# One activation table named for a softmax and the inverse root behind it, and seven steps of the weight differences one slot apart in place of two

## The chip, the cores and the metric

The kernel runs on one core of a Trainium2 chip. The metric is the device time of one execution in microseconds, from the first to the last instruction and what the launch adds around them; times given for a kernel are the median of several runs. In the profile the engines are called PE (TensorE, matmul), PEld (its weight loads), DVE (VectorE), ACT (ScalarE), POOL (GpSimd) and SP (SyncE, which issues the DMAs here).

## The reference

A transformer block with parallel branches: the input, plus sliding-window attention of its layer norm, plus a dense layer with Mish, also of the layer norm.

```python
x = A_x                                   # 1 x 2048 x 576
xn = _layernorm(x, axis=-1)
# attention: 32 heads of 18, window of 8 keys, 2 positions apart
qkv = xn @ wqkv
logits = einsum(q, k at pos - 2*w) * scale ; masked where pos - 2*w < 0
attn = _softmax(logits, axis=-1)
a = (attn @ v) @ wo
# dense -> Mish -> dense, 4608 wide
h = xn @ w1 + b1
act = h * tanh(softplus(h))
b = act @ w2
return x + a + b
```

All of it is in float32.

## The kernel before, in words

**Two halves of tokens.** The 2048 tokens are worked in two halves (`hf` 0 and 1) of 1024, each in two blocks of 512. Every float32 operand of a matmul is split into a high part, cast by ScalarE (`copy` to float32r), and a low part, the difference that VectorE or GpSimd subtracts; a product is then three matmuls. To save matmuls the first dense layer, the output projection and a part of the q/k/v projection are computed in a Strassen-like way, from sums and differences of blocks of the weights and of the tokens.

**The plan.** Everything is put into a list of slots, `plan`. A slot holds TensorE's work of one step: `q` and `z` (q/k/v projection), `m` (first dense layer, `m1_part`: 512-wide products into `h` banks), `p` (second dense layer, `m2_pair`: two `po` tiles of 24 matmuls together, each then added to the accumulator `acc` by VectorE in `add_out`, L663). There are two `po` buffers, so the third of a row of `po` tiles waits until VectorE has read the first. One index `q` of the dense layers takes ten slots, six `m` and four `p` in turn; `spot(hf, q, i)` is the i-th of them. Other work is hung on slots with `before(slot, function)`. When the plan is written out, a slot first runs what is in `soon` (left there by the slot ahead), then what was hung on it, then its own work with what was held back (`pend`, the Mish activations of the products). Each engine runs its instructions in exactly the order in which they are written out.

**Attention** runs beside the dense layers, in steps that are spread evenly over the slots (`attention`, a generator). For a pair of heads GpSimd multiplies q with the keys (`pr`, L474), VectorE reduces to logits `L` (L479), adds a mask, subtracts the maximum, ScalarE takes the exponential (L497, through `soon`), VectorE normalises (L501 to L503), GpSimd multiplies with the values (`pv`, L510) and VectorE reduces that to `og` (L516). Behind the exponential of pair 4 of the first half, `root1` (L126) takes the inverse roots of the second half's variances: a logarithm (L127) and an exponential (L128) of eight values for each partition.

**Activation tables.** ScalarE holds one set of activation functions at a time. The program that builds the kernel puts an ACT_TABLE_LOAD ahead of an activation whose function is not in the set that was loaded last. A set can also be named and loaded explicitly (`preload_act_table_set`, used at L46). Mish (L618) is in another set than the exponential, so there is a load ahead of the softmax's exponential and one ahead of the next Mish.

**The weight differences.** In the second half, groups 2 and 3 of the q/k/v projection use differences of blocks of `wqkv` (`z_part`): with row halves 1 and 2 and column groups 2 and 3 as B11 to B22, T3 = B22 - B12, T1 = B12 - B11, T2 = B22 - T1 and T4 = B21 - T2 (`ZT`, L313). They are made during the first half, for two sets of rows (k = 0, 1). A difference has these steps: `z_load` (a DMA), `z_sum` (GpSimd, L335), `z_high` (ScalarE's cast, L339), `z_low` (VectorE, L343, in place), `z_keep` (two DMAs to DRAM, L347 and L348). T1, T2 and T4 are written over B12, B22 and B21, so the rows call them `zB`; the high parts are `zhT`. All these tiles come from a pool of five, `xn`. A table (L1109 to L1113) says which steps go where: entry n stands on slot `spot(0, 9, 4) + 30 * k + 2 * n` (L1116). Entries 10 to 16 are, in order: write T1; sum T4 and high T2; low T2; high T4; low T4; write T2; write T4.

Of the kernel before, what the change touches and what calls it, by code (L numbers as in the profile page):

```python
# [36 lines left out]
def block_kernel(ctx: ExitStack, tc: tile.TileContext, x, wq, wo, w1, b1, w2, mask, out):  # L37
    nc = tc.nc
# [91 lines left out]
    def newton1():  # L130
        newton(rs1, ve1, y1, nc.gpsimd)
        nc.gpsimd.tensor_mul(nm1, mv1[:, :, 0:1], rs1)
        nc.gpsimd.tensor_scalar(nm1, nm1, -1.0, None, op0=ALU.mult)
# [294 lines left out]
    def load_kv(hf, i, part):  # L428
        g, u = divmod(i, UQ)
        t = sb.tile([P, TJ + HALO, CU], F32, tag="kv", bufs=4, name=f"kv{part}_{hf}_{i}")  # L430
        src = kv_d[g][part * UQ + u, hf * SH, 0:1]
        nc.sync.dma_start(
            t.rearrange("p t c -> p (t c)"),
            bass.AP(tensor=src.tensor, offset=src.offset, ap=[[TJ * CU, P], [1, (TJ + HALO) * CU]]))
        return t

    def load_kq(hf, i):
        g, u = divmod(i, UQ)
        k = load_kv(hf, i, 0)
        q = sb.tile([P, TJ, CU], F32, tag="q", bufs=2, name=f"q_{hf}_{i}")  # L440
        nc.sync.dma_start(q, q_d[g][u, hf * SH:(hf + 1) * SH, :]
                          .rearrange("(p j) c -> p j c", j=TJ))
        return k, q

    def win(kv, c0, cn, j0, jn):
        base = kv[:, j0, c0:c0 + 1]
        return bass.AP(tensor=base.tensor, offset=base.offset,
                       ap=[list(base.ap[0]), [CU, jn], [DIL * CU, W], [1, cn]])

    pend, soon = [], []  # L450

    def attention(hf):
        kqs = [load_kq(hf, k) for k in range(PU)]
        yield
        behind = [None]

        def flush():
            if behind[0] is not None:
                behind[0]()
                behind[0] = None  # L460

        for pair in range(NQ * UQ // PU):
            n = f"{hf}_{pair}"
            vs, nxt = [], []
            L = sb.tile([P, PU, TJ, W, 2], F32, tag="L", bufs=2, name=f"L_{n}")
            hj = TJ // 2
            for k, (kt, q) in enumerate(kqs):
                for c in range(2):
                    flush()
                    pr = sb.tile([P, hj, W, CU], F32, tag="pr", bufs=2, name=f"pr_{n}_{k}_{c}")  # L470
                    j0 = c * hj
                    hh = hj // 2
                    for x in range(0, hj, hh):
                        nc.gpsimd.tensor_tensor(  # L474
                            out=pr[:, x:x + hh], in0=q[:, j0 + x:j0 + x + hh, None, :].to_broadcast([P, hh, W, CU]),
                            in1=win(kt, 0, CU, j0 + x, hh), op=ALU.mult)

                    def red(pr=pr, k=k, j0=j0, L=L):
                        nc.vector.tensor_reduce(  # L479
                            L[:, k, j0:j0 + hj].rearrange("p j w h -> p (j w h)"),  # L480
                            pr.rearrange("p j w (h d) -> p (j w h) d", h=2), axis=AX, op=ALU.add)
                    behind[0] = red
                    if k == 0:
                        vs.append(load_kv(hf, pair * PU + c, 1))
                    yield
            flush()
            if hf == 0:
                lm = L[0:2].rearrange("p k j w h -> p k (j w h)")
                nc.vector.tensor_add(lm, lm, mk[:, None, :].to_broadcast([2, PU, TJ * W * 2]))
            m = sb.tile([P, PU * TJ, 2], F32, tag="m", bufs=2, name=f"m_{n}")  # L490
            Lf = L.rearrange("p k j w h -> p (k j) w h")
            Lt = Lf.rearrange("p j w h -> p j h w")
            nc.vector.tensor_reduce(m, Lt, axis=AX, op=ALU.max)
            mb = m[:, :, None, :].to_broadcast([P, PU * TJ, W, 2])
            nc.vector.tensor_sub(Lf, Lf, mb)
            Ls = L.rearrange("p k j w h -> p (k j w h)")
            soon.append(lambda Ls=Ls: nc.scalar.activation(Ls, Ls, AF.Exp, scale=SCALE))  # L497
            if (hf, pair) == (0, 4):
                soon.append(root1)
            yield  # L500
            nc.vector.tensor_reduce(m, Lt, axis=AX, op=ALU.add)  # L501
            nc.vector.reciprocal(m, m)
            nc.vector.tensor_mul(Lf, Lf, mb)  # L503
            og = sb.tile([P, TJ, PU * CU], F32, tag="og", bufs=1, name=f"og_{n}")
            for k, vt in enumerate(vs):
                for h in range(2):
                    flush()
                    pr = sb.tile([P, TJ, DH, W], F32, tag="pr", bufs=2, name=f"pv_{n}_{k}_{h}")
                    for x in range(0, TJ, hj):
                        nc.gpsimd.tensor_tensor(  # L510
                            out=pr[:, x:x + hj].rearrange("p j d w -> p j w d"),
                            in0=L[:, k, x:x + hj, :, h:h + 1].to_broadcast([P, hj, W, DH]),
                            in1=win(vt, h * DH, DH, x, hj), op=ALU.mult)

                    def red(pr=pr, og=og, c0=k * CU + h * DH, last=(k, h) == (PU - 1, 1), pair=pair):
                        nc.vector.tensor_reduce(og[:, :, c0:c0 + DH], pr, axis=AX, op=ALU.add)  # L516
                        if last:
                            nc.sync.dma_start(
                                o_d[hf][:, pair * PU * CU:(pair + 1) * PU * CU]
                                .rearrange("(p j) c -> p j c", j=TJ), og)  # L520
                    behind[0] = red
                    if (hf, pair, k, h) == (0, 4, 0, 1):
                        newton1()
                    if k == 0 and (pair + 1) * PU + h < NQ * UQ:
                        nxt.append(load_kq(hf, (pair + 1) * PU + h))
                    yield
            kqs = nxt
        flush()
        yield
# [386 lines left out]
    def before(i, fn):  # L916
        plan[max(i, 0)][1].append(fn)
# [154 lines left out]
    def spot(hf, q, i):  # L1072
        return at["s", hf, q, i]

    for q in range(NP):
        if q == 0:
            i = at["q", 0, 3, 1, 0]
            ps_ = dict(raw=i - 3, sums=i - 1, wa=i, wc=i + 1, t0=i + 2, t1=i + 4)
        elif q == 1:
            i = at["q", 0, 3, 0, 0]  # L1080
# [15 lines left out]
    i = spot(0, NP - 1, 0)  # L1096
# [5 lines left out]
    i = at["q", 1, 0, 1, 1]  # L1102
# [4 lines left out]
    i = spot(0, 9, 4)  # L1107
    for k in range(2):
        for n, steps in enumerate((  # L1109
# [4 lines left out]
            for kind, name in steps:  # L1114
                f = dict(l=z_load, s=z_sum, h=z_high, o=z_low, k=z_keep)[kind]
                before(i + 30 * k + 2 * n, lambda f=f, name=name, k=k: f(name, k))  # L1116
    for q in range(NP):
        if q == 0:
            i = at["z", JB - 1, 0]
            ps_ = dict(wa=i - 7, t0=i - 6, t1=i - 5, wc=i - 4)  # L1120
        elif q == 1:
            i = spot(1, 0, 0)
# [9 lines left out]
    i = at["q", 0, 1, 1, 0]  # L1132
# [3 lines left out]
    i = at["q", 0, 3, 1, 0]  # L1136
# [5 lines left out]
    i = at["q", 1, 0, 1, 1]  # L1142
    for n in range(8):
        c, k = divmod(n, 4)
# [7 lines left out]
    for n in range(0, JB, 2):  # L1152
        i = at["q", 0, 1, 0, n]
# [4 lines left out]
    for n in range(TJ):  # L1158
        i = spot(0, 2 + n, 2)
# [3 lines left out]
    i = spot(0, NP - 2, 0)  # L1163
# [26 lines left out]
    def spread(hf, a, b):  # L1190
        before(a - 4, lambda: (att.__setitem__(hf, attention(hf)), next(att[hf])))
        k = a - 1
        for n in range(ASTEPS + 1):
            t = T[a] + n * (T[b] - T[a]) / (ASTEPS + 1)
            k = next(k for k in range(k + 1, len(plan)) if T[k + 1] > t and ok[k])
            before(k, lambda: next(att[hf], None))
# [5 lines left out]
    i = spot(1, NP - 1, 0)  # L1202
# [77 lines left out]
```

## Time and profile before

| what | value |
|---|---|
| median of 3 runs | 1140.36 us (1140.2 to 1140.48) |
| the profiled execution | 1140.93 us |
| its span, first to last instruction | 1138.8 us |
| mean granted TensorE clock | 0.997 |
| ACT_TABLE_LOADs, mean | 1283 ns |

Of these loads 16 stand ahead of a Mish (L618), 15 ahead of a softmax's exponential (L497), and one each at L46, L127 and L128. A row of a timeline has the start in us from the start of the span, the duration, the engine and line, what it writes and reads, shapes and a count of merged instructions; in brackets stands how long the engine was idle ahead of it and what ended that. Buffer numbers are left out in rows of the trace.

### The profile page before, as it was taken

The numbers are of one execution on the slowest core, as the hardware profiler recorded it, in microseconds if no ns is written. First come the engines' busy times: TensorE is split into PE (matmuls) and PEld (weight loads), VectorE is DVE, ScalarE is ACT, GpSimd is POOL, SyncE is SP. The second block draws the span as 40 slices with busy tenths as digits, with TensorE's granted clock in tenths as the row PEclk, the third lists the DMA queues.
The fourth block names the chain that finished last, engine by engine and source line by source line (L and its number), as shares of the span: only waits on it lengthen the run. The fifth ranks groups of instructions, "written<-read, shape, count | busy, mean of one in ns | idle before, by whom it ended". The sixth has DMA issues, their size and how long they took to land.

```text
span 1138.8 us, 17953 instructions
## 1 busy us (share of the span) xinstructions
PE 1125.9 (99%) x6726; PEld 1038.2 (91%) x6726; DVE 738.4 (65%) x1017; ACT 474.1 (42%) x845; POOL 725.9 (64%) x593
## 2 busy tenths in 40 slices
PE   8999999999999899999999999999999999999998
PEld 7998999989999799999999899999999999999998
DVE  6366777788887778877534265554555555556876
ACT  5544544354544535455232432324233342324332
POOL 2487877676689586885683475565664657577432
PEclk9999999999999999999999999999999999999999
DMA  6898767665668576666685984455535454653263
GB/s 203 279 316 306 245 242 262 240 233 211 216 223 303 192 279 228 235 253 211 204 302 179 295 325 167 161 184 210 187 136 191 148 210 144 236 197 105 88 215 110
DMA packets 126923, 246.87 MB, mean 217 GB/s; under 512 B 28754, under 2 KB 66932, under 8 KB 126836
## 3 DMA queue, kind: packets, MB, share of 16 engines
q1 hardware_dynamic: 126836, 245.72, 61.8%
q8 instruction: 53, 0.87, 0.3%
q14 instruction: 34, 0.28, 0.1%
HBM read 148.29 MB, written 97.39 MB: 216 GB/s over the span
## 4 chain that ended last, share of the span: by engine, by line
PE 94%; DVE 3%; ACT 1%; DMA 1%; issue 1%; SPq 0%; DVEq 0%; ACTq 0%
PE po L674 39%; PE h L595 29%; PE pq L289 11%; PE h L601 5%; PE o L828 4%; PE z L387 3%; DVE acc L663 0%; DMA acc<-in_x 0%; PE ta L73 0%; DVE L L479 0%; PE ot L709 0%; PE ot L725 0%; DVE st L110 0%; DVE t L253 0%; DMA kept_w<-w 0%
## 5 line engine op out<-in xcount | busy, mean ns | idle before, releaser
L674 PEld LDWEIGHTS po<-w,act 128*128 128x128 f32 x3456 | 476.2, 189 | 17.2 <-DVE acc L663 6.1
L674 PE MATMUL po<-w,act 128*128 128x288 f32 x3456 | 485.0, 296 | 4.5 <-DVE acc L663 4.4
L663 DVE TENSOR_TENSOR acc<-po,acc 128x576 f32<-128x576 f32 x288 | 215.8, 755 | 178.9 <-PE po L674 176.6
L621 POOL TENSOR_TENSOR act<-c,act 128x512 fp32r<-128x512 f32 x108 | 140.5, 1301 | 224.7 <-ACT act L620 202.1
L474 POOL TENSOR_TENSOR pr<-q,kv 128x576 f32<-128x576 f32 x128 | 191.6, 1520 | 33.0 <-DMA q<-q_d 27.4
L510 POOL TENSOR_TENSOR pv<-L,kv 128x576 f32<-128x576 f32 x128 | 175.7, 1466 | 30.9 <-DVE L L503 20.1
L606 ACT COPY c<-h 128x512 f32<-128x512 f32 x108 | 63.4, 587 | 223.5 <-PE h L601 137.9
L618 ACT ACTIVATE c<-c,b1c 128x512 f32<-128x512 f32 x108 | 78.3, 725 | 178.3 <-DVE c L617 177.8
L289 PE MATMUL pq<-wq,xt 128*128 128x432 f32 x672 | 136.4, 361 | 1.9 <-ACT xt L79 1.8
L289 PEld LDWEIGHTS pq<-wq,xt 128*128 128x128 f32 x672 | 125.0, 188 | 8.8 <-ACT xt L79 2.8
L617 DVE TENSOR_TENSOR c<-h,c 128x512 f32<-128x512 f32 x108 | 74.0, 687 | 72.3 <-PE h L601 36.6
L595 PE MATMUL h<-S,t 128*128 128x512 f32 x432 | 111.3, 393 | 0.0
L595 PE MATMUL h<-xt,t 128*128 128x512 f32 x432 | 110.7, 391 | 0.2 <-DVE c L617 0.2
L595 PE MATMUL h<-xt,wa 128*128 128x512 f32 x432 | 104.2, 390 | 0.0
L595 PEld LDWEIGHTS h<-xt,wa 128*128 128x128 f32 x432 | 81.0, 188 | 17.1
L479 DVE TENSOR_REDUCE L<-pr 128x64 f32<-128x1152 f32 x64 | 85.8, 1341 | 15.9 <-POOL pr L474 15.7
L595 PEld LDWEIGHTS h<-xt,t 128*128 128x128 f32 x432 | 79.2, 188 | 15.5 <-DVE c L617 0.7
L516 DVE TENSOR_REDUCE og<-pv 128x144 f32<-128x1152 f32 x64 | 85.8, 1340 | 8.0 <-POOL pv L510 7.9
L595 PEld LDWEIGHTS h<-S,t 128*128 128x128 f32 x432 | 77.3, 188 | 13.3
L620 ACT CAST act<-c 128x512 fp32r<-128x512 f32 x108 | 67.1, 621 | 4.7 <-PE po L674 0.3
L595 PE MATMUL h<-S,wc 128*128 128x512 f32 x216 | 55.9, 394 | 0.0
L621 POOL TENSOR_TENSOR act<-mn,act 128x512 fp32r<-128x512 f32 x36 | 48.1, 1335 | 6.1 <-ACT act L620 4.7
(179 smaller groups left out, 1235.3 us busy)
## 6 DMA issues: line engine op xcount, KB each, us to landing
kv<-kv_d SPq DMA_DIRECT2D x64, 396.0 KB, 5.7
kept_w<-w SPq DMA_DIRECT2D x36, 576.0 KB, 5.8
w<-kept_w SPq DMA_DIRECT2D x36, 576.0 KB, 5.9
kept_t<-t SPq DMA_DIRECT2D x36, 512.0 KB, 4.8
t<-kept_t SPq DMA_DIRECT2D x36, 512.0 KB, 6.2
rw<-in_w SPq DMA_DIRECT2D x36, 320.0 KB, 4.3
kept_wa<-wa SPq DMA_DIRECT2D x18, 640.0 KB, 6.5
wa<-kept_wa SPq DMA_DIRECT2D x18, 640.0 KB, 5.1
```

The lines of the kernel that those rows point to most:

```text
L289: nc.tensor.matmul(pq[:, 0:432], XT[:, xi, tok], wt[wi][:, hl, 0:432], start=i == 0, stop=i == len(seq) - 1)
L474: nc.gpsimd.tensor_tensor(out=pr[:, x:x + hh], in0=q[:, j0 + x:j0 + x + hh, None, :].to_broadcast([P, hh, W, CU]), in1=win(kt, 0, CU, j0 + ...
L479: nc.vector.tensor_reduce(L[:, k, j0:j0 + hj].rearrange("p j w h -> p (j w h)"), pr.rearrange("p j w (h d) -> p (j w h) d", h=2), axis=AX, ...
L510: nc.gpsimd.tensor_tensor(out=pr[:, x:x + hj].rearrange("p j d w -> p j w d"), in0=L[:, k, x:x + hj, :, h:h + 1].to_broadcast([P, hj, W, DH]),
L516: nc.vector.tensor_reduce(og[:, :, c0:c0 + DH], pr, axis=AX, op=ALU.add)
L595: nc.tensor.matmul(ph, wt[:, wl, wk * P:(wk + 1) * P], X[:, xs, :], start=first and i == 0, stop=last and i == len(seq) - 1, skip_group_ch ...
L617: nc.vector.tensor_tensor(out=t, in0=ph, in1=t, op=ALU.add)
L618: nc.scalar.activation(t, ph if fresh else t, AF.Mish, bias=b1c[:, f:f + 1])
L620: nc.scalar.copy(a[:, 0, :], t)
L621: nc.gpsimd.tensor_tensor(out=a[:, 1, :], in0=t, in1=a[:, 0, :].bitcast(F32), op=ALU.subtract)
L663: nc.vector.tensor_add(t.rearrange("p (c d) -> p c d", c=2), po[:, :, 0:HC], t.rearrange("p (c d) -> p c d", c=2))
L674: nc.tensor.matmul(po[:, c, 0:HC], acts[hf, q, b, j][:, al, tok], done["w2", hf, 2 * q + j][:, wl, c * HC:(c + 1) * HC], start=i == 0, sto ...
```

## The change

Two edits. For pair 4 of the first half, the table set that holds both the logarithm and the exponential is loaded by name ahead of the softmax's exponential. And for k = 0, entries 10 to 16 of the table stand on the slots `i` + 19, 20, 22, 23, 25, 26 and 27 in place of 20, 22, 24, 26, 28, 30 and 32. For k = 1 nothing moves.

```diff
             Ls = L.rearrange("p k j w h -> p (k j w h)")
+            if (hf, pair) == (0, 4):
+                soon.append(lambda: nc.scalar.preload_act_table_set("natural_log_exp_and_others"))
             soon.append(lambda Ls=Ls: nc.scalar.activation(Ls, Ls, AF.Exp, scale=SCALE))
             if (hf, pair) == (0, 4):
                 soon.append(root1)
...
                 f = dict(l=z_load, s=z_sum, h=z_high, o=z_low, k=z_keep)[kind]
-                before(i + 30 * k + 2 * n, lambda f=f, name=name, k=k: f(name, k))
+                before(i + (30 + 2 * n if k else 2 * n if n < 10 else (19, 20, 22, 23, 25, 26, 27)[n - 10]), lambda f=f, name=name, k=k: f(name, k))
```

The two added lines move the numbers of all later lines by 2 in rows of the changed kernel.

In ScalarE's rows around pair 4's softmax (L_0_4 are its logits, rs1 and ve1 belong to the inverse root, c21 and c22 are products that wait for Mish, zhT2 and zhT4 the high parts of T2 and T4) there stood before:

```order
L252 CAST wc_0_12_4058<-rw1_25_3889 128x384
L606 COPY c22_0_11_4105<-h1_0_11_3978 128x512
L339 CAST zhT2_0_4108<-zB22_0_3537 128x432
...
L252 CAST t1_0_12_4145<-tt1_12_3962 128x512
L497 ACT_TABLE_LOAD
L497 ACTIVATE L_0_4_3780<-L_0_4_3780 128x256
L127 ACT_TABLE_LOAD
L127 ACTIVATE rs1_104<-ve1_105 128x8
L128 ACT_TABLE_LOAD
L128 ACTIVATE rs1_104<-rs1_104 128x8
L618 ACT_TABLE_LOAD
L618 ACTIVATE c21_0_11_4052<-c21_0_11_4052,b1c_122 128x512
```

and now:

```order
L252 CAST wc_0_12_4061<-rw1_25_3889 128x384
L339 CAST zhT2_0_4065<-zB22_0_3537 128x432
L608 COPY c22_0_11_4108<-h1_0_11_3978 128x512
...
L252 CAST t1_0_12_4146<-tt1_12_3962 128x512
L339 CAST zhT4_0_4152<-zB21_0_3968 128x432
L498 ACT_TABLE_LOAD
L499 ACTIVATE L_0_4_3780<-L_0_4_3780 128x256
L127 ACTIVATE rs1_104<-ve1_105 128x8
L128 ACTIVATE rs1_104<-rs1_104 128x8
L620 ACT_TABLE_LOAD
L620 ACTIVATE c21_0_11_4055<-c21_0_11_4055,b1c_122 128x512
```

The two loads ahead of L127 and L128 are gone. T2's cast has moved ahead of one COPY, and T4's, which stood behind the next Mish and two casts of w2, has moved ahead of the softmax's table load.

In VectorE's rows from that softmax to the acc addition of the pair `po_0_11_1` (w2, wa and t1 are low parts of weights, og the reduction of pv) there stood before:

```order
L253 TENSOR_TENSOR t1_0_12_4145<-tt1_12_3962,t1_0_12_4145 128x512
L343 TENSOR_TENSOR zB22_0_3537<-zB22_0_3537,zhT2_0_4108 128x432
L617 TENSOR_TENSOR c21_0_11_4052<-h3_0_11_4006,c21_0_11_4052 128x512
...
L663 TENSOR_TENSOR acc_0_0_3_173<-po_0_10_0_3_4190,acc_0_0_3_173 128x576
L501 TENSOR_REDUCE m_0_4_4153<-L_0_4_3780 128x32
...
L516 TENSOR_REDUCE og_0_4_4209<-pv_0_4_0_0_4210 128x8x18
L253 TENSOR_TENSOR w2_0_24_4227<-rw2_24_4095,w2_0_24_4227 128x576
L617 TENSOR_TENSOR c11_0_12_4262<-h2_0_12_4264,c11_0_12_4262 128x512
L253 TENSOR_TENSOR wa_0_13_4276<-rw1_26_4147,wa_0_13_4276 128x640
L343 TENSOR_TENSOR zB21_0_3968<-zB21_0_3968,zhT4_0_4235 128x432
L663 TENSOR_TENSOR acc_0_1_0_183<-po_0_11_1_0_4292,acc_0_1_0_183 128x576
```

and now:

```order
L253 TENSOR_TENSOR t1_0_12_4146<-tt1_12_3962,t1_0_12_4146 128x512
L619 TENSOR_TENSOR c21_0_11_4055<-h3_0_11_4006,c21_0_11_4055 128x512
...
L665 TENSOR_TENSOR acc_0_0_3_173<-po_0_10_0_3_4193,acc_0_0_3_173 128x576
L343 TENSOR_TENSOR zB21_0_3968<-zB21_0_3968,zhT4_0_4152 128x432
L503 TENSOR_REDUCE m_0_4_4156<-L_0_4_3780 128x32
...
L518 TENSOR_REDUCE og_0_4_4213<-pv_0_4_0_0_4214 128x8x18
L253 TENSOR_TENSOR w2_0_24_4231<-rw2_24_4098,w2_0_24_4231 128x576
L619 TENSOR_TENSOR c11_0_12_4267<-h2_0_12_4269,c11_0_12_4267 128x512
L253 TENSOR_TENSOR wa_0_13_4281<-rw1_26_4148,wa_0_13_4281 128x640
L665 TENSOR_TENSOR acc_0_1_0_183<-po_0_11_1_0_4299,acc_0_1_0_183 128x576
```

T4's low part (zB21) no longer stands between og and the acc addition but ahead of the softmax's sum. T2's low part (zB22) has left this stretch; it stands some rows earlier, ahead of the addition to c22.

In SyncE's queue, from the write of w2_23, there stood before:

```order
L260 DMA kept_w2_23_4320<-w2_0_23_4204 128x1152
L260 DMA kept_w2_24_4336<-w2_0_24_4227 128x1152
L197 DMA rw2_25_4338<-in_w2 128x576
L347 DMA kept_T2_0_4343<-zhT2_0_4108 128x432
L348 DMA kept_T2_0_4343<-zB22_0_3537 128x432
...
L260 DMA kept_wa_13_4380<-wa_0_13_4276 128x1280
L197 DMA rw2_26_4383<-in_w2 128x576
L347 DMA kept_T4_0_4395<-zhT4_0_4235 128x432
L348 DMA kept_T4_0_4395<-zB21_0_3968 128x432
```

and now:

```order
L347 DMA kept_T2_0_4239<-zhT2_0_4065 128x432
L348 DMA kept_T2_0_4239<-zB22_0_3537 128x432
L432 DMA kv0_0_11_4252<-kv_d2_128 128x792
L441 DMA q_0_11_4254<-q_d2_132 128x288
L260 DMA kept_t1_12_4278<-t1_0_12_4146 128x1024
L347 DMA kept_T4_0_4283<-zhT4_0_4152 128x432
L348 DMA kept_T4_0_4283<-zB21_0_3968 128x432
L260 DMA kept_w2_23_4327<-w2_0_23_4207 128x1152
```

The writes of T2 and T4 have moved ahead of the write of w2_23. T1's pair of writes has moved likewise, ahead of the write of w2_22 and one load (rw2_23). On GpSimd and TensorE the order of instructions is the same as before.

## The prediction

> **What bounds the kernel.** I read the page's busy times first, then TensorE's waits, then the timeline around the longest of them.
>
> ```profile
> span 1138.8 us, 17953 instructions
> ...
> PE 1125.9 (99%) x6726; PEld 1038.2 (91%) x6726; DVE 738.4 (65%) x1017; ACT 474.1 (42%) x845; POOL 725.9 (64%) x593
> ```
>
> TensorE is busy for all but 12.9 us of the span. No other engine reaches two thirds. An edit that adds or removes no matmul can therefore gain only where TensorE waits or runs slowly.
>
> ```profile
> PE po L674 <- DVE acc L663: 4.4, 2, 4.2
> PE pq L289 <- ACT xt L79: 1.8, 2, 1.2
> ```
>
> (Who waited for whom: us in total, times, longest.) One wait of 4.2 us is by far the longest. Here it is in TensorE's timeline (start, duration, engine and line; in brackets the idle time ahead and what ended it):
>
> ```profile
> 371.82 3.35 PE L674 MATMUL po<-w,act 128*128 128x288 f32 x24
> 375.01 1.55 PE L595 MATMUL h<-xt,t 128*128 128x512 f32 x6
> ...
> 386.44 3.35 PE L674 MATMUL po<-w,act 128*128 128x288 f32 x24
> 389.62 1.54 PE L595 MATMUL h<-S,t 128*128 128x512 f32 x6
> 395.37 5.66 PE L674 MATMUL po<-w,act 128*128 128x288 f32 x24 [4.20 <-DVE acc L663]
> 400.87 1.55 PE L595 MATMUL h<-S,t 128*128 128x512 f32 x6
> ...
> 402.73 3.35 PE L674 MATMUL po<-w,act 128*128 128x288 f32 x24
> ```
>
> TensorE stops at 395.37 - 4.20 = 391.17: the pair at 386.44 filled both po buffers, and the next pair needs the first of them read by VectorE's acc addition. The reader should also see a second cost: the 24 matmuls behind the gap take 400.87 - 395.37 = 5.50 us, the same 24 at 371.82 take 375.01 - 371.82 = 3.19. That is 2.31 us more. The windows say why (span of the window, its length, busy time of each engine with instruction counts, granted TensorE clock, DMA share, GB/s):
>
> ```profile
> 5.00:10.00 5.00, 2.77 (x21) 2.16 (x19) 3.13 (x13) 4.28 (x12) 3.73 (x6) 1.00 1.02 359
> 391.00:392.00 1.00, 0.17 (x1) 0.00 (x0) 1.00 (x2) 0.00 (x0) 0.92 (x2) 1.00 0.00 0
> 393.00:394.00 1.00, 0.00 (x0) 0.00 (x0) 1.00 (x2) 0.97 (x3) 1.00 (x1) 0.74 1.10 378
> 399.00:400.00 1.00, 1.00 (x6) 1.00 (x5) 0.41 (x1) 0.00 (x0) 1.00 (x1) 0.50 0.94 364
> 400.00:401.00 1.00, 1.00 (x8) 1.00 (x7) 0.00 (x0) 0.00 (x0) 1.00 (x2) 0.84 1.09 271
> ```
>
> The clock halves inside 393 to 394 (0.74 there, so at about 393.5, 2.3 us into the gap) and returns at about 400.3. **The gap thus costs 4.20 + 2.31 = 6.51 us**, and that is the most that this change can give.
>
> **What makes the gap.** VectorE first, since its acc addition ends the wait:
>
> ```profile
> 372.64 0.69 DVE L617 TENSOR_TENSOR c<-h,c 128x512 f32<-128x512 f32 x1 [0.54 <-ACT c L606]
> ...
> 379.11 0.60 DVE L343 TENSOR_TENSOR zB<-zB,zhT 128x432 fp32r<-128x432 f32 x1
> ...
> 380.23 1.41 DVE L663 TENSOR_TENSOR acc<-po,acc 128x576 f32<-128x576 f32 x2
> 381.56 0.41 DVE L501 TENSOR_REDUCE m<-L 128x32 f32<-128x256 f32 x1
> ...
> 382.38 0.43 DVE L503 TENSOR_TENSOR L<-L,m 128x256 f32<-128x256 f32 x1
> ...
> 389.24 1.35 DVE L516 TENSOR_REDUCE og<-pv 128x144 f32<-128x1152 f32 x1 [2.48 <-POOL pv L510]
> 390.51 1.29 DVE L253 TENSOR_TENSOR w<-rw,w 128x576 fp32r<-128x576 f32 x1
> ...
> 393.06 1.58 DVE L343 TENSOR_TENSOR zB<-zB,zhT 128x432 fp32r<-128x432 f32 x1
> 394.57 1.41 DVE L663 TENSOR_TENSOR acc<-po,acc 128x576 f32<-128x576 f32 x2
> ...
> 397.16 0.67 DVE L253 TENSOR_TENSOR t<-tt,t 128x512 fp32r<-128x512 f32 x1
> ```
>
> From 389.24 on VectorE works without a pause up to the acc addition at 394.57, and one step of that run is T4's low part (the zB row at 393.06). The run starts late because the og reduction at 389.24 waits for GpSimd's pv product. GpSimd and ScalarE:
>
> ```profile
> 384.85 1.30 POOL L621 TENSOR_TENSOR act<-c,act 128x512 fp32r<-128x512 f32 x1 [8.73 <-ACT act L620]
> 386.10 3.10 POOL L510 TENSOR_TENSOR pv<-L,kv 128x576 f32<-128x576 f32 x2
> ...
> 392.36 3.40 POOL L510 TENSOR_TENSOR pv<-L,kv 128x576 f32<-128x576 f32 x2
> ```
>
> ```profile
> 372.02 0.59 ACT L606 COPY c<-h 128x512 f32<-128x512 f32 x1 [4.05 <-PE h L601]
> 372.50 0.56 ACT L339 CAST zhT<-zB 128x432 fp32r<-128x432 f32 x1
> ...
> 375.28 1.28 ACT L497 ACT_TABLE_LOAD   x1
> 378.62 0.42 ACT L497 ACTIVATE L<-L 128x256 f32<-128x256 f32 x1 [2.06 <-DVE L L495]
> 379.06 1.28 ACT L127 ACT_TABLE_LOAD   x1
> ...
> 380.58 1.28 ACT L128 ACT_TABLE_LOAD   x1
> ...
> 382.10 1.28 ACT L618 ACT_TABLE_LOAD   x1
> ...
> 384.15 0.62 ACT L620 CAST act<-c 128x512 fp32r<-128x512 f32 x1
> ```
>
> GpSimd's pv stands behind an act product that waits 8.73 us for ScalarE's cast at 384.15, and that cast stands behind four table loads, three of them back to back from 379.06.
>
> **The change, part by part.**
>
> *Table loads.* The order rows show the loads ahead of L127 and L128 gone, the first one still ahead of the exponential. The loads leave 2 x 1.28 = 2.56 us. Cast, act product, pv and og reduction start 2.56 earlier: og at 389.24 - 2.56 = 386.68. Late next is VectorE's L at 382.38, which pv also needs: it has 386.10 - 2.56 - (382.38 + 0.43) = 0.73 us to spare.
>
> [...]
>
> *T4's low part* (moved from 393.06 to behind the acc additions at 380.23). It frees 394.57 - 393.06 = 1.51 us ahead of the acc addition that TensorE awaits. In its new place it delays L. Bounds: nothing, if something else were later anyway, and 1.58, its duration beside GpSimd's pv. I take 0.60, the row at 379.11, since GpSimd is idle there as it was for that row (8.73 us before 384.85). The step it displaces helps: T2's low part, the 0.60 row at 379.11, leaves the same stretch. So L moves by about nothing; with 1.58 it would be about 1 us late, 0.25 beyond its spare time.
>
> *T2's low part* goes ahead of the addition at 372.64, where VectorE idles 0.54 us: cost 0.06 at 0.60, about 1 at 1.58. Without that cover it would hold the softmax.
>
> *The two casts* (T2's, T4's) on ScalarE: 0.56 us each (the row at 372.50 is T2's). T2's now falls in the 4.05 us ahead of the COPY at 372.02. T4's comes ahead of the first table load, with 2.06 us idle behind that load. Both cost nothing while those gaps stand.
>
> *The writes* (two DMAs each for T1, T2, T4, on SyncE's queue). T1's pass one kept_w2 and one rw2 load, T2's pass two loads, a kept_t1, two kept_w2 and a rw2 load, T4's pass kept_w2_23 to rw2_26. SyncE may now stand on T4's low part, until about 382; what is queued behind, kept_w2_23, needs a VectorE result from after that point. No TensorE operand is among them, and the loads passed are for the next head pair: cost 0. No GpSimd instruction changes place.
>
> **The sum.** The acc addition starts at 394.57 - 2.56 - 1.51 = 390.50. TensorE resumed 395.37 - 394.57 = 0.80 after its start, so at 391.30, against 391.17: a gap of 0.13 is left, 4.07 saved. A gap that short leaves the clock alone: in 5 to 10 us TensorE idles 2.23 of 5.00 in pieces of at most 1.2, at clock 1.00. So the 2.31 go too: **6.38 us**. The span becomes 1132.4. The profiled execution took 1140.93, 2.13 more than its span and 0.57 above the median of 1140.36; 6.38 off the median is **1134.0**.
>
> Next at risk is the pair behind: it moves up 6.4 us, GpSimd only 2.56. The pv at 392.36 would end at 393.20; og (1.26), t (0.67) and the acc addition to its release (0.80) end at 395.93. TensorE needs it 402.73 - 395.37 - 2.31 = 5.05 after 391.30, at 396.35. Spare: 0.42.
>
> **Rivals.**
>
> *A smaller gap stays (1135.3).* If a moved low part takes 1.58 or a GpSimd product is slow, about 1.3 us of waiting is left. Spares of 0.42 and 0.73 speak for it, idle GpSimd against.
>
> *The clock halves all the same (1136.3).* If DMA load caused it (share 1.10 at 393), only the 4.07 come back. Against: share 1.02 in 5 to 10 at clock 1.00.
>
> *A wait takes its place (1138.4).* If GpSimd's second pv does not move up, the release comes at 395.93 + 2.56, a gap of 2.1, and the clock may halve again: 6.38 - 2.1 - 2.31 = 2.0 saved. Against: the act product there waits for ScalarE alone, and 8.73 us of idle time is ahead of it.
>
> [...]
>
> *Slower (1143).* T4's cast fills a tile that T1's write must have left, and the softmax and everything behind it on ScalarE now queue behind that cast.
>
> ```profile
> 363.81 0.88 SPq L347 DMA_DIRECT2D kept_T<-zhT  x1
> ...
> DMA to landing us min/median/max: 3.9/4.0/4.1
> ```
>
> The write was issued by 364.7 and would land by 368.8. The cast delays the exponential if it lands after 378.62 - 1.28 - 0.56 = 376.8; the gap is as long as before, half clock included, at 376.8 + 4.07 = 380.9, and from 383.2 on the kernel is slower by over 2.3 us. Landing at 384 it would lose 3.1. That is 15 us later than the row gives, and the write now issues earlier.
>
> *It doesn't do what it says (1140.4).* Should ScalarE load its table anyway, only T4's 1.51 would remain, perhaps lost in the clock. The order rows speak against.
>
> **How the numbers follow.** Forecast (5.8 to 6.6 saved) 0.73; smaller gap 0.10; clock 0.05; wait in its place 0.06; slower 0.04; no effect 0.02. About 0.2%, 2.3 us, is what a measurement here can tell from no change. Faster: 0.73 + 0.10 + 0.05 = 0.88; same 0.06 + 0.02 = 0.08; slower 0.04. The range goes from 1133.3 (all 6.51 saved, and 0.57, the distance of the profiled execution from the median) to 1136.8 (the clock rival, and as much).
>
> **What would show it.** Right: two table loads between the softmax's exponential row and the next Mish row become one, the og reduction starts near 386.7, TensorE's longest wait is about 1 us, clock 1.00 throughout, 24 matmuls in 3.19 us. Wrong: a po wait above 1 us near 391 or 396, a window below clock 1.00, or ScalarE idle ahead of T4's cast.

## The result, and the profile after

| | before | changed |
|---|---|---|
| median, runs of both on the same chips | 1139.88 us (1139.0 to 1140.48, 6 runs) | 1133.62 us (1133.23 to 1133.76, 6 runs) |
| profiled execution | 1140.93 us | 1133.61 us |
| its span | 1138.8 us | 1131.8 us |
| mean granted TensorE clock | 0.997 | 1.0 |

The changed kernel takes 0.9945 of the time of before (95% interval 0.9932 to 0.9958), 6.26 us less by the medians. The page's busy times:

```profile
PE 1124.5 (99%) x6726; PEld 1037.1 (92%) x6726; DVE 739.2 (65%) x1017; ACT 471.1 (42%) x843; POOL 725.4 (64%) x593
```

The count of ScalarE's instructions went from 845 to 843: two loads are gone and nothing else. TensorE's waits, in the same columns as before:

```profile
PE warm L62 <- POOL ident masks.py:199: 1.3, 1, 1.3
PE pq L289 <- ACT xt L79: 1.0, 2, 0.6
PE po L676 <- DVE acc L665: 0.4, 2, 0.2
```

The wait for the acc addition, 4.2 us and far ahead of all others before, is 0.2 us. The timeline at the place of the gap:

```profile
385.83 3.35 PE L676 MATMUL po<-w,act 128*128 128x288 f32 x24
389.01 1.54 PE L597 MATMUL h<-S,t 128*128 128x512 f32 x6
390.79 3.46 PE L676 MATMUL po<-w,act 128*128 128x288 f32 x24 [0.23 <-DVE acc L665]
394.08 1.55 PE L597 MATMUL h<-S,t 128*128 128x512 f32 x6
395.46 0.62 PE L603 MATMUL h<-xt,wc 128*128 128x512 f32 x2
395.92 3.35 PE L676 MATMUL po<-w,act 128*128 128x288 f32 x24
```

The gap is 0.23 us, and the 24 matmuls behind it take 394.08 - 390.79 = 3.29 us; they took 5.50 before. So 3.97 of the 4.20 and 2.21 of the 2.31 came back, 6.18 together. The rest of the 7.0 us between the two spans lies elsewhere: 0.61 us are there before the gap (the pair begins at 385.83, before at 386.44), from shorter waits in the first 40 us. Across the nine kept traces that pair begins anywhere from 385.66 to 386.44. The windows around the place:

```profile
386.00:391.00 5.00, 4.77 (x31) 4.17 (x31) 4.82 (x6) 1.60 (x3) 4.92 (x6) 1.00 0.31 110
391.00:392.00 1.00, 1.00 (x9) 1.00 (x9) 0.40 (x1) 1.00 (x3) 1.00 (x2) 1.00 0.88 277
392.00:394.00 2.00, 2.00 (x17) 2.00 (x17) 1.55 (x2) 0.16 (x1) 1.58 (x8) 1.00 0.98 272
394.00:396.00 2.00, 2.00 (x11) 1.66 (x10) 2.00 (x4) 0.00 (x0) 2.00 (x2) 1.00 0.97 385
```

The clock column stays at 1.00, with a DMA share of 0.88 to 0.98 from 391 on; before, it was 0.50 at a share of 0.94 (399 to 400). ScalarE:

```profile
374.56 0.55 ACT L339 CAST zhT<-zB 128x432 fp32r<-128x432 f32 x1
375.12 1.28 ACT L498 ACT_TABLE_LOAD   x1
378.01 0.42 ACT L499 ACTIVATE L<-L 128x256 f32<-128x256 f32 x1 [1.61 <-DVE L L495]
378.34 0.19 ACT L127 ACTIVATE rs<-ve 128x8 f32<-128x8 f32 x1
378.56 0.21 ACT L128 ACTIVATE rs<-rs 128x8 f32<-128x8 f32 x1
378.79 1.28 ACT L620 ACT_TABLE_LOAD   x1
380.08 0.72 ACT L620 ACTIVATE c<-c,b1c 128x512 f32<-128x512 f32 x1
```

The softmax's exponential, the logarithm and the root's exponential run one behind another on one table. T4's cast has come ahead of the load, and 1.61 us of idle time still stand behind that load. GpSimd and VectorE:

```profile
381.54 1.30 POOL L623 TENSOR_TENSOR act<-c,act 128x512 fp32r<-128x512 f32 x1 [6.03 <-ACT act L622]
383.19 2.95 POOL L512 TENSOR_TENSOR pv<-L,kv 128x576 f32<-128x576 f32 x2 [0.36 <-DVE L L505]
```

```profile
380.43 0.59 DVE L343 TENSOR_TENSOR zB<-zB,zhT 128x432 fp32r<-128x432 f32 x1
380.94 0.41 DVE L503 TENSOR_REDUCE m<-L 128x32 f32<-128x256 f32 x1
381.39 0.35 DVE L504 RECIPROCAL m<-m 128x32 f32<-128x32 f32 x1
381.78 1.34 DVE L505 TENSOR_TENSOR L<-L,m 128x256 f32<-128x256 f32 x1
383.04 0.75 DVE L253 TENSOR_TENSOR w<-rw,w 128x576 fp32r<-128x576 f32 x1
386.18 1.35 DVE L518 TENSOR_REDUCE og<-pv 128x144 f32<-128x1152 f32 x1 [2.39 <-POOL pv L512]
...
389.99 1.41 DVE L665 TENSOR_TENSOR acc<-po,acc 128x576 f32<-128x576 f32 x2
...
394.35 1.41 DVE L665 TENSOR_TENSOR acc<-po,acc 128x576 f32<-128x576 f32 x2
```

One row on the way to pv is longer than it was: the normalisation of L (L505) takes 1.34 us, 0.43 before. It now runs beside GpSimd's act product (381.54 to 382.84), and pv waits 0.36 us for it.

### The profile page after: what moved, and what is told of

The parts are those of the page before. It is cut to its first block, busy times and chain, and to the rows that moved or that the text cites. A ratio compares the mean times of both kernels' runs of the same rounds, so it can differ in the third digit from the quotient of the medians.

```text
span 1131.8 us, 17954 instructions
## 1 busy us (share of the span) xinstructions
PE 1124.5 (99%) x6726; PEld 1037.1 (92%) x6726; DVE 739.2 (65%) x1017; ACT 471.1 (42%) x843; POOL 725.4 (64%) x593
## 4 chain that ended last, share of the span: by engine, by line
PE 94%; DVE 3%; ACT 1%; DMA 1%; issue 1%; POOL 0%; SPq 0%; DVEq 0%; POOLq 0%; ACTq 0%
PE po L676 39%; PE h L597 29%; PE pq L289 11%; PE h L603 6%; PE o L830 4%; PE z L387 3%; PE ta L73 0%; DMA o<-o_d 0%; DVE acc L665 0%; DVE L L479 0%; PE ot L711 0%; PE ot L727 0%; DVE st L110 0%; DMA acc<-in_x 0%; POOL pv L512 0%
```

## The experiments

Times are medians; each kernel was timed beside runs of before on the same chip, whose medians were 1139.95 us (18 runs) for the first four and 1140.39 us (13 runs) for the last three. The diffs are cut where `...` stands. They are against the changed kernel, except that of the shorter gap, which is against the kernel with the gap put back.

### The table alone

```diff
-                before(i + (30 + 2 * n if k else 2 * n if n < 10 else (19, 20, 22, 23, 25, 26, 27)[n - 10]), lambda ...
+                before(i + 30 * k + 2 * n, lambda ...
```

> The table set is named, the seven steps stand where they stood before. My theory: T4's low part is back ahead of the awaited acc addition and costs 1.5 us there, so TensorE's gap is 0.2 + 1.5 = 1.7 us; the clock stays at 1.00, since it fell only 2.3 us into the gap of before; the kernel is 4.7 us faster than before. Rival 1, any gap of over a microsecond halves the clock: 2.2 us more lost, 2.5 us faster than before. Rival 2, the table loads carry all of the gain and the steps nothing: gap 0.2 us, 6.3 us faster than before.

Measured: 1135.06 us (1134.89 to 1135.33, 5 runs), 4.89 us faster than before, ratio 0.9958 (0.9945 to 0.9970); clock 1.0 in all five. TensorE and VectorE at the place:

```profile
392.58 3.46 PE L676 MATMUL po<-w,act 128*128 128x288 f32 x24 [1.74 <-DVE acc L665]
395.88 1.54 PE L597 MATMUL h<-S,t 128*128 128x512 f32 x6
```

```profile
390.28 1.58 DVE L343 TENSOR_TENSOR zB<-zB,zhT 128x432 fp32r<-128x432 f32 x1
391.78 1.41 DVE L665 TENSOR_TENSOR acc<-po,acc 128x576 f32<-128x576 f32 x2
```

T4's low part is back ahead of the acc addition and costs 391.78 - 390.28 = 1.50 us there; the gap is 1.74 and the matmuls behind it run at full clock (3.30 us). Both rivals are out.

### The steps alone

```diff
-            if (hf, pair) == (0, 4):
-                soon.append(lambda: nc.scalar.preload_act_table_set("natural_log_exp_and_others"))
```

> The seven steps stand as in the changed kernel, the softmax and the root load their tables as before (four loads). My theory: only T4's 1.5 us leave the run ahead of the acc addition, the gap is 4.2 - 1.5 = 2.7 us, longer than the 2.3 us after which the clock fell, so the 24 matmuls behind it still take about 5.4 us instead of 3.2: 1.5 us faster than before. Rival 1, a gap of 2.7 us leaves the clock alone: 3.7 us faster. Rival 2, the steps do nothing: gap 4.2 us, the time of before.

Measured: 1136.92 us (1135.9 to 1138.03, 8 runs), ratio 0.9975 (0.9964 to 0.9985). The gap in the profiled execution:

```profile
393.42 3.46 PE L674 MATMUL po<-w,act 128*128 128x288 f32 x24 [2.63 <-DVE acc L663]
396.72 1.54 PE L595 MATMUL h<-S,t 128*128 128x512 f32 x6
```

The gap is 2.63 us, near the 2.7 expected, but the matmuls take 3.30 us at full clock in this execution. The eight executions fall into two groups: four at 1135.9 to 1136.51 with clock 1.0 and four at 1137.33 to 1138.03 with clock 0.998. So neither the theory nor rival 1 holds for every execution: with this gap the clock fell in four of the eight. That the clock falls whenever the gap is longer than 2.3 us was wrong.

### The gap put back by other work

```diff
+    scr = const.tile([P, 432], F32, name="scr")
...
+    nc.vector.memset(scr, 0.0)
...
+    def extra():
+        for r in range(2):
+            nc.vector.tensor_tensor(out=scr, in0=scr, in1=scr, op=ALU.subtract)
+    before(spot(0, 12, 2), extra)
```

> The changed kernel with two more VectorE subtractions of T4's size (128 x 432, on a scratch tile that nothing reads) ahead of the awaited acc addition. My theory: 1.5 us each beside GpSimd's pv, so a gap of 0.2 + 3.0 = 3.2 us comes back although table loads and steps stay as changed, and with it the half clock: 3.0 + 2.2 = 5.2 us slower than the changed kernel, 1 us faster than before. Rival, the clock of before fell because of something else in that stretch (DMA load): gap 3.2 us, clock 1.00, 3.0 us slower than the changed kernel.

Measured: 1138.31 us (1136.24 to 1139.56, 10 runs). In the profiled execution:

```profile
394.12 3.45 PE L676 MATMUL po<-w,act 128*128 128x288 f32 x24 [3.24 <-DVE acc L665]
397.41 1.55 PE L597 MATMUL h<-S,t 128*128 128x512 f32 x6
```

The gap is 3.24 us, 0.23 + 3.01, and the two subtractions took 3.02 us (from 390.30 to the acc addition at 393.32): VectorE's work ahead of that addition passed to TensorE one to one here. Again there are two groups: four executions at 1136.24 to 1137.2 (clock 1.0), mean 1136.68, 3.06 above the changed kernel: the gap alone. Six at 1138.06 to 1139.56 (clock 0.997 or 0.998), mean 1138.86, 2.18 more: the gap and the half clock. DMA load alone did not bring the clock down: the profiled execution has DMA shares of 0.96 to 1.08 in its windows from 390 to 394 and a clock of 1.00 in all of them. Nor are the removed table loads needed for the half clock, which came back without them in six executions.

### Of the steps, T4's two parts alone

```diff
-                before(i + (30 + 2 * n if k else 2 * n if n < 10 else (19, 20, 22, 23, 25, 26, 27)[n - 10]), lambda ...
+                before(i + (23 if (k, n) == (0, 13) else 25 if (k, n) == (0, 14) else 30 * k + 2 * n), lambda ...
```

> The changed kernel, but of the seven steps only T4's high and low part are moved; the sum, T2's two parts and the writes stand as before. My theory: T2's low part (0.6 us) is back between the softmax's maximum and its sum, the normalised L is 0.6 us later, and since GpSimd's pv already waits 0.36 us for it in the changed kernel, the gap is 0.2 + 0.6 = 0.8 us, clock 1.00. Rival, L is not what pv waits for: gap 0.2 us.

One execution: 1133.12 us, gap 0.23 us as in the changed kernel, so this theory fell. The rival's number came true, but not its reason: pv does wait for L, by 0.37 us. VectorE and GpSimd there:

```profile
380.78 0.60 DVE L343 TENSOR_TENSOR zB<-zB,zhT 128x432 fp32r<-128x432 f32 x1
...
382.13 0.81 DVE L505 TENSOR_TENSOR L<-L,m 128x256 f32<-128x256 f32 x1
```

```profile
381.37 1.29 POOL L623 TENSOR_TENSOR act<-c,act 128x512 fp32r<-128x512 f32 x1 [6.03 <-ACT act L622]
383.02 2.96 POOL L512 TENSOR_TENSOR pv<-L,kv 128x576 f32<-128x576 f32 x2 [0.37 <-DVE L L505]
```

The normalisation starts 0.76 us behind the start of the act product (0.24 in the changed kernel), yet it ends 0.28 us behind the product's end in both (382.94 against 382.66, and 383.12 against 382.84). It starts at different points of the product and ends equally far behind it, and pv follows. The same kernel was then timed:

> The kernel of the look before it (table set named; of the seven steps only T4's high and low part moved), now timed. Theory after that look: T4's place is all that the steps give, since the gap was 0.23 us there too; within 0.3 us of the changed kernel, 6.2 us faster than before. Rival, the five other steps are worth something that one look does not show (loads and writes that are out of the way earlier): over 0.5 us slower than the changed kernel.

Measured: 1133.97 us (1133.48 to 1134.45, 5 runs), ratio 0.9947 (0.9934 to 0.9961); the changed kernel had 0.9945. That is 6.42 us faster than its own runs of before, against 6.26 for the changed kernel. The five other steps give nothing that can be measured.

### A shorter gap

```diff
     def extra():
-        for r in range(2):
-            nc.vector.tensor_tensor(out=scr, in0=scr, in1=scr, op=ALU.subtract)
+        for c in (432, 116):
+            nc.vector.tensor_tensor(out=scr[:, 0:c], in0=scr[:, 0:c], in1=scr[:, 0:c], op=ALU.subtract)
```

> The changed kernel with one more subtraction of T4's size and one of 116 columns ahead of the awaited acc addition; a gap between that of the table alone (1.74 us, clock 1.00 in 5 of 5 executions) and that of the steps alone (2.63 us, half clock in 4 of 8). [...]

The gap missed its size. The two added subtractions and the pv beside them (durations in ns in the first line: shortest, median, longest):

```profile
L1123 DVE TENSOR_TENSOR scr<-scr x2: 1144/1368/1593, 389.9 to 391.5; 128x432 f32<-128x432 f32 x1, 128x116 f32<-128x116 f32 x1
389.19 3.38 POOL L512 TENSOR_TENSOR pv<-L,kv 128x576 f32<-128x576 f32 x2
```

The 116 columns took 1.14 us, from 391.5 to 392.65, which is 0.08 us behind the end of GpSimd's pv at 392.57, and the gap was 2.94 us. So what the clock does with a gap of 2 us was not measured. Measured: 1137.69 us, three executions of nine at 1135.98 to 1136.15 and six at 1137.41 to 1138.53. The profiled one is of the second kind and shows how the clock goes:

```profile
390.00:391.00 1.00, 0.44 (x2) 0.01 (x1) 1.00 (x1) 0.98 (x2) 1.00 (x2) 1.00 1.15 359
...
392.00:393.00 1.00, 0.00 (x0) 0.00 (x0) 1.00 (x2) 0.06 (x1) 0.91 (x3) 1.00 1.10 270
393.00:394.00 1.00, 0.63 (x4) 0.63 (x5) 1.00 (x3) 0.00 (x0) 0.67 (x4) 0.93 0.89 230
394.00:395.00 1.00, 1.00 (x6) 1.00 (x5) 1.00 (x1) 0.00 (x0) 1.00 (x2) 0.50 0.92 328
...
397.00:398.00 1.00, 1.00 (x8) 1.00 (x8) 0.02 (x1) 0.00 (x0) 1.00 (x2) 0.87 1.02 379
```

TensorE idles from 390.44 to 393.37, but the clock falls only at about 393.86 (0.93 over the window 393 to 394), when TensorE is at work again, and returns at 397.26: 3.40 us later. In the kernel before it fell at about 393.5 and returned at 400.3, 6.8 us later, twice that.

### T4's low part behind the normalisation

```diff
-                ... else (19, 20, 22, 23, 25, 26, 27)[n - 10]), lambda ...
+                ... else (19, 20, 22, 23, 26, 26, 27)[n - 10]), lambda ...
```

> The changed kernel, but T4's low part stands one slot later, behind the softmax's normalisation and the low part of w2_23, in VectorE's idle time ahead of og. Theory: the normalisation of L, which took 1.34 us in the changed kernel (0.43 before) because GpSimd's act product ran beside it, starts 0.5 us earlier, ahead of that product, and takes 0.43 again; pv no longer waits its 0.36 us, the gap of 0.23 us closes, 0.2 us faster than the changed kernel, which timing can just not tell. Rival, the normalisation is stretched to the end of the act product wherever it starts: pv and the gap as in the changed kernel.

Measured: 1133.2 us (1133.1 to 1134.07, 5 runs), ratio 0.9944 (0.9931 to 0.9956), gap 0.26 us.

```profile
381.19 0.42 DVE L505 TENSOR_TENSOR L<-L,m 128x256 f32<-128x256 f32 x1
382.00 1.39 DVE L253 TENSOR_TENSOR w<-rw,w 128x576 fp32r<-128x576 f32 x1 [0.38 <-ACT w L252]
383.31 1.60 DVE L343 TENSOR_TENSOR zB<-zB,zhT 128x432 fp32r<-128x432 f32 x1
386.14 1.35 DVE L518 TENSOR_REDUCE og<-pv 128x144 f32<-128x1152 f32 x1 [1.22 <-POOL pv L512]
```

```profile
381.47 1.31 POOL L623 TENSOR_TENSOR act<-c,act 128x512 fp32r<-128x512 f32 x1 [6.03 <-ACT act L622]
382.73 3.38 POOL L512 TENSOR_TENSOR pv<-L,kv 128x576 f32<-128x576 f32 x2
```

The theory was right as far as pv's start: the normalisation takes 0.42 us, and pv follows the act product without a wait. Then pv takes 3.38 us instead of 2.95, with two of VectorE's low parts beside it where there was one, and og starts as far behind the act product as in the changed kernel (386.14 - 381.47 = 4.67 against 386.18 - 381.54 = 4.64). What was taken from the one engine was given back by the other, and this version doesn't beat the changed kernel.

## Why the prediction was right

**The bound and the size of the gap.** 6.38 us were forecast, 6.26 were measured by the medians, 6.18 at the place itself. The step on which all rests, that nothing but TensorE's gap and the half clock behind it is to be had here, held: no wait of more than 0.4 us came in elsewhere. It is the saving that has to be compared: the forecast time of 1134.0 was counted from 1140.36, and before took 1139.88 beside the changed kernel.

**The table loads** were put at 2.56 us. Measured against the point where TensorE runs out of work (391.17 before, 390.79 - 0.23 = 390.56 now), og starts 390.56 - 386.18 = 4.38 us ahead of it, before 391.17 - 389.24 = 1.93: 2.45 us gained. By the same count the act product starts 390.56 - 381.54 = 9.02 ahead, before 391.17 - 384.85 = 6.32, so 2.70 earlier. That is 0.14 more than the two loads themselves, as the instructions now overlap a little where a load stood between them (the logarithm starts at 378.34, the exponential ends at 378.43). Pv's wait for the normalisation takes 0.36 from the 2.70, and a pv of 2.95 in place of 3.10 gives 0.15 back. The 0.73 us of spare time counted the normalisation at its 0.43 of before, but it now falls beside the act product and ends 0.28 behind it. The prediction was right that the loads bring pv forward, but wrong that L would have time to spare. That the term came within 0.11 us is partly luck, since neither the 0.14 gained, nor the 0.36 lost, nor the 0.15 given back was costed.

A load takes 1.28 us in the changed kernel too, and behind the one at 378.79 the next instruction starts at once (380.08).

**T4's low part** was put at 1.51 us freed and 0.60 in its new place: 1.50 (the table alone) and 0.59 (the profile after). That T2's low part helps by leaving the stretch was wrong: with it left in, the gap is the same (T4's two parts alone), since the normalisation, started 0.52 us later into the act product, ends 0.28 us behind it all the same. The prediction's own 0.73 us of spare time would also have covered those 0.60. The moved sum, T2's parts and the writes are worth nothing that can be measured, in line with costs of 0.06 us and less.

**The pair behind** had 0.42 us to spare by the prediction. The acc additions are at 394.35 (a row of VectorE's timeline after), the third pair at 395.92: with 0.80 to its release about 0.8 us are left. No wait took the place of the one removed.

**The clock.** That the half clock came from the gap was right (the gap put back by other work), and so was its price, 2.31 forecast and 2.21 measured at the place. The rule used for it, that 2.3 us of idle time suffice, holds only for some executions:

| kernel | gap in the profiled execution | executions with the half clock |
|---|---|---|
| changed | 0.23 us | 0 of 6 |
| table alone | 1.74 us | 0 of 5 |
| steps alone | 2.63 us | 4 of 8 |
| a shorter gap | 2.94 us | 6 of 9 |
| the gap put back | 3.24 us | 6 of 10 |

For the last three the count is by the two groups of times. Of before, with 4.20 us, no execution came near the 1137.6 us or so that it would take without the half clock: the lowest is 1138.82.

For gaps of 2.6 to 3.2 us the length alone does not decide. In the profiled executions:

| kernel | gap | clock | time at half clock |
|---|---|---|---|
| table alone | 1.74 us | 1.00 in all windows from 388 to 401 | none |
| steps alone | 2.63 us | 1.00 in all windows from 388 to 401 | none |
| a shorter gap | 2.94 us | 0.50 from 0.49 us after the gap's end | 3.40 us |
| the gap put back | 3.24 us | 1.00 in all windows from 388 to 401 | none |
| before | 4.20 us | 0.50 from 2.32 us into the gap | 6.83 us |

The gap of 3.24 us passed at full clock and the one of 2.94 us did not. In before TensorE idled for 1.88 us more after the clock had fallen; in the shorter gap it was already at work again when the clock fell. The two traces of before and of the changed kernel also hold the lengths of the stretches at one clock: in before 389.119 us at 1.0, then 6.827 us at 0.5, then 740.692 us at 1.0; in the changed kernel 1126.398 us at 1.0. The three long ones are 57.0, 108.5 and 165.0 times the 6.827 us, so in these two traces all four are whole multiples of half of it, 3.41 us; the clock was low for about as long, 3.40 us, in the shorter gap. What decides whether a gap of 2.6 to 3.2 us brings the clock down was not shown.

**The rivals.** A smaller gap, the clock for another reason, a wait in its place and the late write of T1 all stayed away, and the loads did go. For the write of T1: T4's cast ran at 374.56 with no idle time ahead of it, so it did not wait for that write.

## What to carry to other kernels

Where one engine is busy to 99%, look for the one wait that is left and ask which run of work ends it; here two unrelated edits, 2.45 us on ScalarE and 1.5 us on VectorE, lay on the same run and added up, and only two of the seven moved steps mattered. Count the matmuls behind a gap as well as the gap: their lower clock was a third of what could be gained. And the gaps of 2.63, 2.94 and 3.24 us cost a lower clock in 16 of 27 executions here, so one profile of such a kernel can show either case: look at the clock of all of them.

## What was not expected of the hardware

- VectorE's normalisation of L (256 columns) took 1.34 us in the changed kernel and 0.81 us with T4's two parts alone, started 0.24 and 0.76 us into GpSimd's act product, and it ended 0.28 us behind the product both times. Started 0.28 us ahead of the product (T4's low part behind the normalisation) it took 0.42 us, and 0.43 us in before, where GpSimd was idle. The 116 columns of the shorter gap took 1.14 us and ended 0.08 us behind pv. The low part of w2_23 took 0.75 us where it started at 383.04, ahead of the pv at 383.19, and 1.39 us where it started inside the act product (at 382.00, T4's low part behind the normalisation). Other pairs of instructions were not tried.
- GpSimd's pv took 2.95 us beside one low part of VectorE (changed kernel) and 3.38 us beside two (T4's low part behind the normalisation). How the loss is divided between the two engines was not tried.
- The half clock of TensorE began 2.32 us into the gap of before and lasted 6.83 us. In the shorter gap it began when the gap was already over (at 393.86, work resumed at 393.37) and lasted 3.40 us.
